# The first MLP's tiles one token group after the other, no partial sums in DRAM, a new issue order, operands at other addresses

## The chip, the cores and the metric

The kernel runs on one core of a Trainium2 chip. The metric is the device time of one execution in microseconds (us); lower is better. A measurement is the median of a few runs.

## The reference

Attention with a window of 64 keys, then two MLPs on the 2304 tokens (4 batches of 576, 8 heads of 64; width 512).

```python
attn = softmax(where((rel >= 0) & (rel < 64), q @ k.T / 8, -1e9)) @ v        # per batch and head
x = attn, heads side by side                                                 # 2304 x 512
h = x @ w_in;  x = (h * tanh(softplus(h))) @ w_out                           # 512 -> 2048 -> 512
h = x @ w_in2;  solu = h * softmax(h)                                        # 512 -> 1024
x = ((solu - mean) / sqrt(var + 1e-6) * g_ln) @ w_out2                       # 1024 -> 512
```

## The kernel before

The tokens are cut into five groups of 512, 512, 512, 384 and 384. For each group the attention of its blocks of 64 tokens (in pairs) leaves its output in a tile `xt` (two buffers, so group j+2 needs the one that group j gives back), split into a high and a low half. The first MLP goes through items `(j, f, a, b)` in the list `its`: group j, column tile f of sixteen of 128 columns, tokens a to b of the group. An item is 12 matmuls of `pe_m1` (L950, into `ps_h`), Mish on ScalarE (L960), the split of its result into two halves `g` (on ScalarE or VectorE, L423, L427, L443), then 8 matmuls of `pe_m2` (L984) and 4 of `pe_m2l` (L995) that add to the group's four accumulators `x2`, a PSUM bank each. All of them read both operands as fp32r, one pass.

The order of the items before is: group 0, tiles 0 to 3, in two halves of 256 tokens; group 0, tiles 4 to 7; group 1, tiles 0 to 7; then tiles 8 to 15 of group 0 and of group 1; then groups 2, 3 and 4 with sixteen tiles each. So groups 0 and 1 each close their accumulators twice: behind tile 7 the sums go to DRAM (`part_d`, `store_x2`), and behind tile 15 they are read back (`load_part`) and added on VectorE (`evac_part`, L1010). The finished group goes to DRAM (`x2d`) for the second MLP.

The weights come as 32-bit halves of 64-bit numbers in pieces of one or two tiles (`c_load`, L481, with two staging buffers `st`). ScalarE or GpSimd scale the words (L491 to L500), VectorE joins them (L508, L516), and they are split into a high half (L423, L427) and a low half (L443). From the third group on, attention transposes its scores in blocks through DRAM (`blocks_out`, L375, then `blocks_in`, L381), and so does the second MLP for its second product.

The second MLP takes two tiles of 128 tokens at a time: seven products of 6 matmuls (`b_p`, L1118) with `xs` (on the right side of SBUF) or, for every second pair, `xs_w` (in a weight buffer on the left side) as the stationary operand and `w_in2` as the moving one, then SoLU and the norm, then 24 matmuls of `b_m4` (L1235) for each of the 18 tiles.

Nothing is scheduled by the compiler. A planner in the program (`Schedule`) has all steps with their costs and what they come after; in `run` it takes, step by step, the one that its own clock lets start first, and among those within `PATIENCE` the one with the lowest number in `RANK`. The order in which it takes them is the order on each engine's queue. All DMAs are issued by SP.

SBUF is filled from both sides. From the left, starting at byte 1152 of a partition: `ident`, `mask_n`, `mask_0` (512 bytes each), `g_sb` (32 bytes), the weight buffers, `st`, `xt`, `mc`, `g`, `xs` of the evacuation. From the right, downward from byte 229344: the attention's tiles, later those of the second MLP. All large tiles have multiples of 128 bytes.

## Time and profile before

| | us |
|---|---|
| median of 3 runs | 669.59 |
| lowest and highest run | 665.54, 669.97 |
| the profiled execution, whole | 667.13 |
| its span, first to last instruction | 665.4 |
| PE busy (of the span) | 649.1 |
| DVE, ACT, POOL busy | 423.6, 348.3, 40.9 |

PE is TensorE's matmuls, PEld its weight loads (beside PE), DVE is VectorE, ACT is ScalarE, POOL is GpSimd, SP issues DMAs (its queue is SPq). Busy time is the union of an engine's instructions. Matmuls are pipelined, so the time of one in a stream is read from the distance between starts, as the chain gives it, and not from its own duration.

### The profile page before, as it was taken

The numbers are of one execution on the slowest core, as the hardware profiler recorded it, in microseconds if no ns is written. First come the engines' busy times: TensorE is split into PE (matmuls) and PEld (weight loads), VectorE is DVE, ScalarE is ACT, GpSimd is POOL, SyncE is SP. The second block draws the span as 40 slices with busy tenths as digits, with TensorE's granted clock in tenths as the row PEclk, the third lists the DMA queues.
The fourth block names the chain that finished last, engine by engine and source line by source line (L and its number), as shares of the span: only waits on it lengthen the run. The fifth ranks groups of instructions, "written<-read, shape, count | busy, mean of one in ns | idle before, by whom it ended". The sixth has DMA issues, their size and how long they took to land.

```text
span 665.4 us, 10569 instructions
## 1 busy us (share of the span) xinstructions
PE 649.1 (98%) x4089; PEld 556.8 (84%) x4089; DVE 423.6 (64%) x741; ACT 348.3 (52%) x616; POOL 40.9 (6%) x63
## 2 busy tenths in 40 slices
PE   8899999999999989999999999999998999999997
PEld 6688888878888878788899999999886888788886
DVE  4778887876356656321115655776687988879751
ACT  5989775544344434232123545655576555657532
POOL 2412000000000001000000010000011001110100
PEclk9999999999999999999999999999999999999999
DMA  8874565576068453020044345602216555554562
GB/s 333 332 279 166 163 214 199 181 272 207 1 205 254 145 185 131 32 64 1 0 159 159 108 117 173 210 13 95 80 37 154 189 159 158 173 160 139 174 178 95
DMA packets 56962, 101.36 MB, mean 152 GB/s; under 512 B 5072, under 2 KB 30672, under 8 KB 56912
## 3 DMA queue, kind: packets, MB, share of 16 engines
q1 hardware_dynamic: 56912, 100.69, 46.5%
q8 instruction: 32, 0.52, 0.3%
q14 instruction: 18, 0.15, 0.1%
HBM read 74.45 MB, written 26.21 MB: 151 GB/s over the span
## 4 chain that ended last, share of the span: by engine, by line
PE 77%; DMA 10%; DVE 6%; ACT 3%; SPq 2%; issue 1%; POOL 0%; ACTq 0%; DVEq 0%
PE ps_h L950 26%; PE x L984 18%; PE po L1235 10%; PE x L995 9%; PE pb L1118 9%; DMA t_d<-s 3%; PE ps_o L903 2%; PE ps_s L741 2%; DMA h_b<-t_d 2%; DMA t_d<-y_b 2%; DMA st<-w_in 1%; SPq L381 1%; DMA room_q<-qk 1%; DMA pt<-t_d 1%; DMA xr<-x2d 1%
## 5 line engine op out<-in xcount | busy, mean ns | idle before, releaser
L950 PE MATMUL ps_h<-xt,w 128*128 128x512 f32 (+2 forms) x1008 | 205.4, 359 | 1.2 <-ACT mc L960 1.0
L950 PEld LDWEIGHTS ps_h<-xt,w 128*128 128x128 f32 x1008 | 177.2, 188 | 23.1 <-ACT mc L960 1.9
L984 PE MATMUL x<-g,w 128*128 128x512 f32 (+2 forms) x672 | 146.5, 359 | 1.0 <-DVE g L427 0.6
L984 PEld LDWEIGHTS x<-g,w 128*128 128x128 f32 x672 | 118.8, 188 | 16.3 <-ACT g L423 1.1
L443 DVE SCALAR_TENSOR_TENSOR g<-mc,g 128x512 fp32r<-128x512 f32 (+2 forms) x84 | 51.5, 618 | 94.8 <-ACT g L423 94.3
L1235 PE MATMUL po<-w,lz 128*128 128x512 f32 x432 | 101.4, 391 | 2.6 <-ACT lz L1215 2.5
L1235 PEld LDWEIGHTS po<-w,lz 128*128 128x128 f32 x432 | 80.6, 188 | 21.4 <-ACT lz L1215 4.6
L960 ACT ACTIVATE mc<-ps_h 128x512 f32<-128x512 f32 (+2 forms) x84 | 44.8, 535 | 98.5 <-PE ps_h L950 94.5
L995 PE MATMUL x<-g,w 128*128 128x512 f32 (+2 forms) x336 | 80.8, 362 | 0.0
L423 ACT ACTIVATE g<-mc 128x512 fp32r<-128x512 f32 (+2 forms) x68 | 39.2, 578 | 60.4 <-PE x L995 59.3
L995 PEld LDWEIGHTS x<-g,w 128*128 128x128 f32 x336 | 59.4, 188 | 7.9 <-issue 1.0
L1118 PE MATMUL pb<-w,xs 128*128 128x512 f32 x210 | 51.1, 395 | 0.0
L1118 PEld LDWEIGHTS pb<-w,xs 128*128 128x128 f32 x210 | 39.4, 188 | 9.2
L1118 PE MATMUL pb<-w,xs_w 128*128 128x512 f32 x168 | 39.8, 390 | 0.0
L1118 PEld LDWEIGHTS pb<-w,xs_w 128*128 128x128 f32 x168 | 31.5, 188 | 6.7
L1215 ACT ACTIVATE lz<-h_b 128x512 fp32r<-128x512 f32 x36 | 21.3, 626 | 29.6 <-DMA h_b<-t_d 19.4
L1219 DVE TENSOR_TENSOR lz<-h_b,lz 128x512 fp32r<-128x512 f32 x36 | 24.0, 686 | 17.3 <-ACT lz L1215 17.2
L508 DVE SCALAR_TENSOR_TENSOR st<-st 128x1024 uint32<-128x1024 uint32 x22 | 26.9, 1224 | 10.8 <-ACT st L493 9.2
L844 POOL TENSOR_TENSOR s<-s,rs 128x1024 f32<-128x1024 f32 x6 | 11.5, 1923 | 354.0 <-DMA x2d<-xs 187.3
L435 ACT ACTIVATE v_b<-pb 128x512 f32<-128x512 f32 x33 | 19.6, 595 | 20.0 <-PE pb L1118 18.2
L500 ACT ACTIVATE st<-st 128x1024 uint32<-128x1024 uint32 x22 | 25.4, 1156 | 6.3 <-DMA st<-w_out 6.3
L1150 ACT ACTIVATE e<-h_b,nm 128x1024 f32<-128x1024 f32 x18 | 20.7, 1151 | 9.1 <-DVE nm L1141 8.9
(133 smaller groups left out, 712.5 us busy)
## 6 DMA issues: line engine op xcount, KB each, us to landing
qk<-qk SPq DMA_DIRECT2D x32, 512.0 KB, 5.2
st<-w_out SPq DMA_DIRECT2D x12, 1024.0 KB, 5.7
st<-w_in SPq DMA_DIRECT2D x10, 1024.0 KB, 6.0
t_d<-y_b SPq DMA_DIRECT2D x18, 512.0 KB, 2.8
h_b<-t_d SPq DMA_DIRECT2D x72, 128.0 KB, 3.2
v<-v SPq DMA_DIRECT2D x32, 256.0 KB, 3.7
t_d<-s SPq DMA_DIRECT2D x10, 512.0 KB, 3.3
pt<-t_d SPq DMA_DIRECT2D x40, 128.0 KB, 3.1
```

Of the source, the lines that this page charges most:

```text
L423: nc.scalar.activation(out=hi, in_=x, func=ACTF.Copy, scale=1.0 if g is None else g)
L443: nc.vector.scalar_tensor_tensor(out=lo, in0=x, scalar=1.0 if g is None else g, in1=hi.bitcast(F32), op0=ALU.mult, op1=ALU.subtract)
L500: nc.scalar.activation(out=w, in_=w, func=ACTF.Copy, scale=0.9325 * 2.0**-29)
L508: nc.vector.scalar_tensor_tensor(out=lw, in0=uw, scalar=3, in1=lw, op0=ALU.logical_shift_left, op1=ALU.bitwise_or)
L950: nc.tensor.matmul(out=ps[:, :n], lhsT=w[:, a, k, fs], rhs=x[:, b, k, a0:a1], start=(idx == 0), stop=(idx == len(terms) - 1),)
L960: nc.scalar.activation(out=c[:, :n], in_=ht.pop(i)[:, :n], func=ACTF.Mish)
L984: nc.tensor.matmul(out=acc[j][m][:, a0:a1], lhsT=w[:, a, f % 4, m * P:(m + 1) * P], rhs=g[:, 0, :n], start=(i in opens and a == 0), stop=F ...
L995: nc.tensor.matmul(out=acc[j][m][:, a0:a1], lhsT=w[:, 0, f % 4, m * P:(m + 1) * P], rhs=g[:, 1, :n], start=False, stop=i in closes,)
L1118: nc.tensor.matmul(out=ps, lhsT=x[:, a, ix, k, :], rhs=w[:, k, :], start=first and n == 0, stop=n == len(terms) - 1, skip_group_check=not ...
L1215: nc.scalar.activation(out=lt[t][:, 0, fs].rearrange(SPLIT, i=4), in_=pst[t][:, :, fs], func=ACTF.Copy)
L1219: nc.vector.tensor_tensor(out=lt[t][:, 1, fs].rearrange(SPLIT, i=4), in0=pst[t][:, :, fs], in1=lt[t][:, 0, fs].bitcast(F32).rearrange(SPLI ...
L1235: nc.tensor.matmul(out=po[t], lhsT=lz[:, a, f, :], rhs=wt["w4", f // 4][:, b, f % 4, :], start=(c == 0 and idx == 0), stop=(c == 2 and idx ...
```

## The change

- `its` has all sixteen tiles of group 0 (the first four in halves, as before), then all of group 1, then the rest as before. `CUT`, `part_d`, `load_part` and `evac_part` go; `opens` and `closes` hold five sets of accumulators in place of seven. The places of attention beside the items follow from `its`, and group 2's due times (`BESIDE_AT`) are new.
- `RANK` is new from end to end, and some costs in the planner are new.
- `g_sb` is opened behind the left side's attention tiles in place of among the constants, a tile `pad` of 96 bytes is the first on the right side, and the tile `warm`, read twice in place of once by the warm-up matmuls, is half as large. So the left side's tiles start 32 bytes lower and the right side's 96 bytes lower.

```diff
@@ -26,7 +26,6 @@
 BLK = 64
 LD = 2
 HALF = 4
-CUT = 8
 N_T = 16
 SPLIT = "p f (i c) -> p i f c"
 LAG = 3
@@ -73,7 +72,7 @@
 FIRST_AT = (-247.536, -138.103, 26.663)
 W_STEP = 5.104
 M4_LATER = -89.542
-BESIDE_AT = ((74.191, 100.532), (62.075, 50.39), (-14.947, 89.638), (16.431, 50.986), (-8.343, 27.444))
+BESIDE_AT = ((74.191, 100.532), (62.075, 50.39), (4.0, 24.0), (16.431, 50.986), (-8.343, 27.444))
 BESIDE_PE = 2.411
 PATIENCE = 0.031
 SLACK = 41.257
@@ -93,86 +92,84 @@
 
 
 RANK = (
...
@@ -359,12 +356,9 @@
     x2d = [dram.tile([P, KD, n], F32, name=f"x2d{j}") for j, n in enumerate(GROUPS)]
-    part_d = [dram.tile([P, KD, n], F32, name=f"part{j}") for j, n in enumerate(GROUPS[:2])]
-
     ident = const.tile([P, P], F32, name="ident")
     mask_n = const.tile([P, P], F32, name="mask_n")
     mask_0 = const.tile([P, P], F32, name="mask_0")
-    g_sb = const.tile([P, NF2], F32, name="g_sb")
@@ -408,8 +402,13 @@
     st_p = actx.enter_context(tc.tile_pool(name="st", bufs=2))
     x_p = actx.enter_context(tc.tile_pool(name="x", bufs=2))
     m_p = actx.enter_context(tc.tile_pool(name="m", bufs=2))
+    g_p = actx.enter_context(tc.tile_pool(name="g_ln", bufs=1))
+    g_sb = g_p.tile([P, NF2], F32, name="g_sb")
     ps_x2 = actx.enter_context(tc.tile_pool(name="ps_x2", bufs=KD, space=PSUM))
     ps_h = actx.enter_context(tc.tile_pool(name="ps_h", bufs=2, space=PSUM))
+
+    pad = ctx.enter_context(tc.tile_pool(name="pad", bufs=1, side="right"))
+    pad.tile([P, 24], F32, name="pad")
     tctx = ExitStack()
     ectx = ExitStack()
     ld_p = tctx.enter_context(tc.tile_pool(name="ld", bufs=LD, side="right"))
@@ -586,10 +585,8 @@
     n = GROUPS[0] // 2
     its = [(0, f, o, o + n) for o in (0, n) for f in range(HALF)]
-    its += [(0, f, 0, 2 * n) for f in range(HALF, CUT)]
-    its += [(1, f, 0, GROUPS[1]) for f in range(CUT)]
-    its += [(j, f, 0, GROUPS[j]) for j in range(2) for f in range(CUT, NF)]
-    its += [(j, f, 0, GROUPS[j]) for j in range(2, NG) for f in range(NF)]
+    its += [(0, f, 0, 2 * n) for f in range(HALF, NF)]
+    its += [(j, f, 0, GROUPS[j]) for j in range(1, NG) for f in range(NF)]
     NI = len(its)
     first_of = {}
     for i, it in enumerate(its):
@@ -682,7 +679,7 @@
     def warm_up():
-        w = sm_p.tile([P, 256], BF16, tag="warm", name="warm", bufs=1)
+        w = sm_p.tile([P, P], BF16, tag="warm", name="warm", bufs=1)
         nc.vector.memset(w, 0.0)
         room["warm"] = w
         zeros(ps_h.tile([P, 512], F32, tag="h", name="ps_w"), N_WARM)
@@ -690,7 +687,10 @@
     def zeros(ps, n):
         w = room["warm"]
         for _ in range(n):
-            nc.tensor.matmul(out=ps[:, :256], lhsT=w[:, :P], rhs=w, start=True, stop=True)
+            nc.tensor.matmul(
+                out=ps[:, :256].rearrange("p (a b) -> p a b", a=2), lhsT=w, rhs=w.unsqueeze(1).to_broadcast([P, 2, P]),
+                start=True, stop=True,
+            )
     def bridge(ps):
@@ -927,8 +927,8 @@
-    opens = {i for i, (j, f, a, b) in enumerate(its) if a == 0 and (f == 0 or (f == CUT and j < 2))}
-    closes = {i for i, (j, f, a, b) in enumerate(its) if f == NF - 1 or (f == CUT - 1 and j < 2)}
+    opens = {i for i, (j, f, a, b) in enumerate(its) if a == 0 and f == 0}
+    closes = {i for i, (j, f, a, b) in enumerate(its) if f == NF - 1}
     ht, ct, gt = {}, {}, {}
     acc = {}
@@ -997,20 +997,7 @@
                 start=False, stop=i in closes,
             )
-    out_t, xs_t = {}, {}
-
-    def load_part(j, m):
-        out_t[m] = m_p.tile([P, GMAX], F32, tag="xs", name="xs", bufs=KD)
-        nc.sync.dma_start(out=out_t[m][:, :GROUPS[j]], in_=part_d[j][:, m, :])
-
-    def evac_part(i, m):
-        j, f, _, _ = its[i]
-        n = GROUPS[j]
-        s = out_t.pop(m)
-        nc.vector.scalar_tensor_tensor(
-            out=s[:, :n], in0=acc[j][m][:, :n], scalar=1.0, in1=s[:, :n], op0=ALU.mult, op1=ALU.add
-        )
-        xs_t[m] = s
+    xs_t = {}
     def evac_x2(e, i, m):
         j, f, _, _ = its[i]
@@ -1025,7 +1012,7 @@
     def store_x2(i, m):
         j, f, _, _ = its[i]
         n = GROUPS[j]
-        nc.sync.dma_start(out=(x2d if f == NF - 1 else part_d)[j][:, m, :], in_=xs_t.pop(m)[:, :n])
+        nc.sync.dma_start(out=x2d[j][:, m, :], in_=xs_t.pop(m)[:, :n])
     with tc.manual_schedule():
@@ -1382,7 +1369,7 @@
             mx = step(dict(dve=0.84), t + offs[2], a_max0, n, after=[qk], new=[s, nm], uses=[S, s, nm, room_s])
             e0 = step(dict(act=0.70), t + offs[3], a_exp0, n, (0, 1), after=[mx], uses=[S, s, nm, room_s], table="exp")
             e1 = step(dict(act=0.70), t + offs[4], a_exp0, n, (2, 3), after=[e0], uses=[S, s, nm], table="exp")
-            r = step(dict(dve=0.35), t + offs[5], a_norm, n, after=[e1], new=[rs], uses=[nm, rs])
+            r = step(dict(dve=0.4), t + offs[5], a_norm, n, after=[e1], new=[rs], uses=[nm, rs])
             mu = step(COSTS["mul0"], t + offs[5], a_mul, n, after=[r], uses=[s, rs], two=True)
             tr = step(dict(pe=0.434), t + offs[6], a_tr, n, after=[mu], new=[T], uses=[s, T])
             cp = step(COSTS["pt0"], t + offs[7], a_pt, n, after=[tr], uses=[T, s])
@@ -1405,7 +1392,7 @@
                 mx = step(dict(dve=1.37), t + offs[2], a_max, n, after=[qk], new=[nm], uses=[S, nm])
             else:
                 qk = step(dict(pe=0.88), t + offs[0], a_qk, n, after=lks + pv_of_old, new=[S], uses=ks + [S], mode="qk")
-                sc = step(dict(dve=1.23 if n < N_T else 1.55), t + offs[1], a_scale, n, after=[qk, masks, mask_x] + moved[-1:], new=[s], uses=[S, s])
+                sc = step(dict(dve=1.23 if n < N_T else 1.42), t + offs[1], a_scale, n, after=[qk, masks, mask_x] + moved[-1:], new=[s], uses=[S, s])
                 mx = step(dict(dve=1.2), t + offs[2], a_max, n, after=[sc], new=[nm], uses=[s, nm])
             if n < NM:
                 ex = step(dict(act=1.55), t + offs[4], a_exp2, n, range(NP), after=[mx], new=[s], uses=[S, s, nm], table="exp")
@@ -1418,7 +1405,7 @@
                 su = step(dict(dve=1.23), t + offs[3], a_sub, n, after=[mx], uses=[s, nm])
                 ex = step(dict(act=1.03), t + offs[4], a_exp, n, after=[su], uses=[s], table="exp")
                 sm = step(dict(dve=1.2), t + offs[5], a_sum, n, after=[ex], uses=[s])
-            r = step(dict(dve=0.35), t + offs[5], a_norm, n, after=[sm], new=[rs], uses=[rs])
+            r = step(dict(dve=0.4), t + offs[5], a_norm, n, after=[sm], new=[rs], uses=[rs])
             mu = step(COSTS["mul"], t + offs[6], a_mul, n, after=[r], uses=[s, rs], two=True)
             if n < N_T:
                 tr = step(dict(pe=0.87), t + offs[7], a_tr, n, after=[mu] + pv_last[-1:], new=[T], uses=[s, T])
@@ -1427,10 +1414,10 @@
                 c = [c0, c1]
             else:
                 T = Buf("s2")
-                bl = step(dict(dve=1.13), t + offs[7], a_blocks, n, after=[mu], uses=[s])
+                bl = step(dict(dve=1.25), t + offs[7], a_blocks, n, after=[mu], uses=[s])
                 td = Buf("td")
-                mo = step(dict(dma=1.4), t + offs[8], a_out, n, after=[bl], new=[td, T], uses=[s, td])
-                c0 = step(dict(dma=2.0), t + offs[8], a_in, n, after=[mo], uses=[T, td])
+                mo = step(dict(dma=1.5), t + offs[8], a_out, n, after=[bl], new=[td, T], uses=[s, td])
+                c0 = step(dict(dma=2.6), t + offs[8], a_in, n, after=[mo], uses=[T, td])
                 moved.append(mo)
                 c, s = [c0, c0], T
             finish(n, t, offs[9:], mu, (ws, s), O, c)
@@ -1465,22 +1452,13 @@
             last_m2[:] = [m2]
             m1_of[i], m2_of[i] = m1, m2
             if i in closes:
-                loads, outs_ = [], []
                 for m in range(KD):
-                    part = j < 2 and f == NF - 1
                     xs = Buf("xs")
-                    if part:
-                        loads.append(step(dict(dma=0.7), o[4] - 2.5, load_part, j, m, after=[part_of[j][m], m1_of[i - 3]] + last_out, new=[xs], uses=[xs]))
-                    ev = step(
-                        dict(dve=0.15 + 0.4 * k) if part else COSTS["x2"], o[4] + 1.2, evac_part if part else evac_x2, i, m, after=[m2] + loads[m:m + 1], new=[] if part else [xs],
-                        uses=[xs, acc_of[j][m]],
-                    )
+                    ev = step(COSTS["x2"], o[4] + 1.2, evac_x2, i, m, after=[m2], new=[xs], uses=[xs, acc_of[j][m]])
                     sto = step(dict(dma=0.7), o[4] + 1.3, store_x2, i, m, after=[ev], uses=[xs])
-                    outs_.append(sto)
-                    (part_of if f == CUT - 1 and j < 2 else done_of).setdefault(j, []).append(sto)
-                last_out[:] = outs_
-
-        acc_of, part_of, done_of, last_m2, last_out = {}, {}, {}, [], []
+                    done_of.setdefault(j, []).append(sto)
+
+        acc_of, done_of, last_m2 = {}, {}, []
         U0 = PRE_STEP
         PRE = -(N0 - 1) * U0 - max(PRE_AT) - 0.02
         for n in range(N0):
@@ -1563,7 +1541,7 @@
                     after = after + [vs_[bank][-1]]
                 if ps_:
                     after = after + [ps_[-1]]
-                q = step(dict(pe=1.362), a + P_AT[3], b_p, u, i, after=after, new=[bk[bank]] if first else [], uses=[bk[bank], xs_])
+                q = step(dict(pe=1.4), a + P_AT[3], b_p, u, i, after=after, new=[bk[bank]] if first else [], uses=[bk[bank], xs_])
                 ps_.append(q)
                 xs_last[u % 2] = [q]
                 got[i] = q
@@ -1578,7 +1556,7 @@
                 t = 2 * u + i
                 after = [x for n in vn for x in vs_["v", n]] + ([got[q]] if q is not None else []) + ([cs[t, 0]] if c else [])
                 cs[t, c] = step(
-                    dict(dve=0.84), a + P_AT[5], b_c, u, i, c, after=after + [ob2], new=[hb[t]] if c == 0 else [],
+                    dict(dve=0.72), a + P_AT[5], b_c, u, i, c, after=after + [ob2], new=[hb[t]] if c == 0 else [],
                     uses=[hb[t]] + ([bk[bank]] if bank is not None else []),
                 )
                 for n in vn:
@@ -1595,13 +1573,13 @@
             sq = step(dict(act=1.25), o[2], b_sq, t, after=[sa], uses=[h, y, st])
             va = step(dict(dve=0.28), o[2], b_var, t, after=[sq], uses=[st])
             va = step(dict(pool=1.0), o[3], b_pow, t, after=[va], uses=[st])
-            sh = step(dict(dve=0.3), o[3], b_shift, t, after=[va], uses=[st])
+            sh = step(dict(dve=0.2), o[3], b_shift, t, after=[va], uses=[st])
             z = step(dict(dve=0.82), o[3], b_z, t, after=[sh], uses=[h, st])
             Y, lz = Buf("bty"), Buf("blz")
-            tr = step(dict(dve=1.13), o[4], b_tr, t, after=[z, ob2], new=[Y], uses=[h, Y])
+            tr = step(dict(dve=1.25), o[4], b_tr, t, after=[z, ob2], new=[Y], uses=[h, Y])
             td = Buf("td")
-            mo = step(dict(dma=1.4), o[4], b_out_t, t, after=[tr], new=[td], uses=[Y, td])
-            mv = step(dict(dma=2.0), o[4], b_in_t, t, after=[mo], uses=[h, td])
+            mo = step(dict(dma=1.5), o[4], b_out_t, t, after=[tr], new=[td], uses=[Y, td])
+            mv = step(dict(dma=2.6), o[4], b_in_t, t, after=[mo], uses=[h, td])
             h0 = step(dict(act=0.55), o[5], b_hi, t, 0, after=[mv], new=[lz], uses=[h, lz])
             l0 = step(dict(dve=0.69), o[5], b_lo, t, 0, after=[h0], uses=[h, lz], two=True)
             h1 = step(dict(act=0.55), o[5], b_hi, t, 1, after=[h0], uses=[h, lz])
```

## Rows read from the trace of the kernel before

**Rows 1.** Part 1 of the page: busy us (share of the span) xinstructions.

```profile
PE 649.1 (98%) x4089; PEld 556.8 (84%) x4089; DVE 423.6 (64%) x741; ACT 348.3 (52%) x616; POOL 40.9 (6%) x63
```

**Rows 2.** Stretches; for each engine busy us and (xinstructions), then clock, DMA share, GB/s.

```profile
0.00:33.00 33.00, 27.38 (x336) 21.97 (x336) 20.52 (x43) 25.62 (x87) 10.88 (x22) 1.00 0.90 335
33.00:129.00 96.00, 94.19 (x735) 81.33 (x732) 79.05 (x98) 72.07 (x142) 5.69 (x3) 1.00 0.59 198
129.00:235.90 106.90, 106.64 (x739) 87.08 (x739) 65.99 (x92) 45.13 (x58) 0.00 (x0) 1.00 0.57 185
...
462.00:640.00 178.00, 175.43 (x777) 144.20 (x776) 145.10 (x345) 107.20 (x185) 20.34 (x36) 1.00 0.47 143
640.00:665.40 25.40, 21.60 (x96) 17.55 (x94) 6.10 (x9) 6.12 (x11) 0.00 (x0) 0.99 0.37 115
```

**Rows 3.** Chain of work that ended last: start, us, engine, tile, line, xcount.

```profile
39.79 1.44 PE ps_h L950 x12
...
94.08 19.04 PE ps_h L950 x84
...
412.20 12.48 PE ps_h L950 x72
```

**Rows 4.** Waits of PE, longest first: us in total, times, longest; two of nine, and the last.

```profile
PE po L1235 <- ACT lz L1215: 2.5, 2, 1.7
PE ps_o L903 <- DMA pt<-t_d: 2.1, 2, 1.9
...
PE x L984 <- ACT g L423: 0.4, 1, 0.4
```

**Rows 5.** Part 6 of the page, DMA issues of the partial sums.

```profile
part<-xs SPq DMA_DIRECT2D x8, 256.0 KB, 4.8
xs<-part SPq DMA_DIRECT2D x8, 256.0 KB, 5.0
```

**Rows 6.** Groups by line and form: the add of a partial sum on DVE.

```profile
L1010 DVE SCALAR_TENSOR_TENSOR xs<-x,xs 128x512 f32<-128x512 f32 x8 | 5.3, 686 | 0.1
```

**Rows 7.** Stretches from 0, matmuls of line L950 alone: length, busy us, (xcount).

```profile
0.00:129.20 129.20, 46.65 (x240) 1.00 0.67 233
...
0.00:150.70 150.70, 57.96 (x288) 1.00 0.69 238
0.00:156.30 156.30, 63.52 (x312) 1.00 0.69 238
```

**Rows 8.** DVE in order of time, last step of a weight piece: start us, us.

```profile
73.21 1.22 DVE L443 SCALAR_TENSOR_TENSOR w<-st,w 128x1024 fp32r<-128x1024 f32 x1
...
86.96 1.22 DVE L443 SCALAR_TENSOR_TENSOR w<-st,w 128x1024 fp32r<-128x1024 f32 x1
...
127.15 1.22 DVE L443 SCALAR_TENSOR_TENSOR w<-st,w 128x1024 fp32r<-128x1024 f32 x1
...
133.36 1.23 DVE L443 SCALAR_TENSOR_TENSOR w<-st,w 128x1024 fp32r<-128x1024 f32 x1
```

**Rows 9.** PE in order of time, three rows that have a wait in brackets.

```profile
246.09 1.15 PE L903 MATMUL ps_o<-pt,v 128*64 128x64 f32 x32 [1.89 <-DMA pt<-t_d]
...
507.48 7.87 PE L1235 MATMUL po<-w,lz 128*128 128x512 f32 x32 [1.67 <-ACT lz L1215]
...
566.61 3.93 PE L1235 MATMUL po<-w,lz 128*128 128x512 f32 x16 [0.87 <-ACT lz L1215]
```

**Rows 10.** Waits of SP's queue (issuing of DMAs).

```profile
SPq L481 <- DVE w L443: 60.8, 10, 12.4
```

**Rows 11.** PE in order of time at the start of the second MLP.

```profile
473.78 8.56 PE L1118 MATMUL pb<-w,xs 128*128 128x512 f32 x36
482.18 9.71 PE L1118 MATMUL pb<-w,xs_w 128*128 128x512 f32 x42
491.73 8.56 PE L1118 MATMUL pb<-w,xs 128*128 128x512 f32 x36
```

**Rows 12.** Part 5 of the page, the product with xs.

```profile
L1118 PE MATMUL pb<-w,xs 128*128 128x512 f32 x210 | 51.1, 395 | 0.0
```

158 rows, old and new, of the table RANK are left out of this document.

## The prediction, made before the changed kernel was run

> **What bounds the kernel now.** I read the page's busy shares first, then the 20-us-and-longer stretches, then the list of what TensorE waited for, then the chain of work that ended last. TensorE is busy 649.1 of 665.4 us [rows 1], at a granted clock of 1.00 in every stretch, the higher of its two levels (2.4 GHz) [rows 2]. The chain, too, is TensorE work for long stretches without a break [rows 3]. So the reader should not look for a big wait; the question is what TensorE's own 649 us consist of and where its 16 us of idle time lie. By the stretches 5.6 us of idle time lie ahead of 33 us, 1.8 between 33 and 129 us, 2.6 in the second MLP, and 3.8 behind the last matmul (the output's copy and store) [rows 2]. The list of waits holds nine entries of 0.4 to 2.5 us each, and none of them names a partial sum, its load or its store [rows 4].
>
> The matmuls themselves: there are 84 passes of 24 in the first MLP, 378 in the second one's first product and 432 in its last, 2826 in all, of which 1866 have 512 columns, 768 have 384 and 192 have 256 (from the loops). Where the chain runs through many of them in a row, one takes 19.04/84 = 226.7 ns at 512 columns, 12.48/72 = 173.3 ns at 384 and 1.44/12 = 120 ns at 256 [rows 3]. Each is 13.3 ns above its columns at 2.4 GHz (213.3, 160.0, 106.7). Sum: 1866 x 0.2267 + 768 x 0.1733 + 192 x 0.120 = 579 us. The diff leaves every one of these 2826 in place, with the same shapes. So the time can only move by the idle time, by the 13.3 ns, or by new waits.
>
> **Part 1, no partial sums.** Removed: 8 stores and 8 loads of 256 KB [rows 5], and the 8 adds on VectorE (5.3 us busy, 0.69 each) [rows 6]; the other evacuations stay. No wait of TensorE is put down to them [rows 4], VectorE is busy for only 79 of the 96 us ahead of 129 us and less behind [rows 2]. I cost this at 0; the cover is the TensorE queue itself, and without it one add would be worth 0.7 us. Closing a set of accumulators happens five times in place of seven. There TensorE bridges the evacuation with the next tiles' first matmuls, and no wait shows there either: 0.
>
> **Part 2, the order of the tiles.** This is where a new wait could come from. Tile 8 of group 0 now follows tile 7 directly, so weight pieces for tiles 8 to 15 are wanted earlier. Before, tile 8's first matmul is number 241 of its line, at 129.2 us, tile 12's number 289, at 150.7, tile 14's number 313, at 156.3 [rows 7]. The last step of converting the pieces (the subtraction that writes the low half) starts at 86.96 us for tiles 8 and 9 and at 127.15 and 133.36 us for tiles 12 to 15 of w_in, 1.2 us each [rows 8]. So before there are 41, 22 and 22 us of slack.
>
> After: tile 8 comes where group 1's first tile stood, at 93.8 us, or some 6 us earlier, since group 1's attention (four pairs of blocks, each three bursts on TensorE, of which the last is 1.15 us [rows 9]; by that size some 3.4 us a pair, an estimate) is now spread over twice as many tiles. That is 88 to 94 us against 88.2 us. From there two tiles cost TensorE 2 x 24 x 0.2267 = 10.9 us, while two tiles need two pieces, one of each matrix, and the pieces come every (133.36 - 73.21)/9 = 6.7 us (ten such rows from the first to the last of [rows 8]), 13.4 us for both. The pace is set by a ring: two staging buffers, a load that waits for the last VectorE step of the piece before (60.8 us of such waits in the queue that issues the DMAs [rows 10]). Supply is thus a little slower than demand and the slack is eaten. TensorE's work from 33 us to the end of group 0 is 8 half tiles of 24 x 0.120 = 23.0 us, 12 tiles of 5.44 = 65.3 us and about 15 us of attention (four to five pairs): earliest end 136 us. With the last piece in at 134.6 us and the second products of two tiles (5.4 us) behind it, the end is 140 us: up to 3.5 us lost. Against that, TensorE may run group 1's first products meanwhile, w_in's last pieces can swap with w_out's, and the VectorE work of group 1's attention moves later. Bounds: 0 and +3.5 for this; I take +1.5. Queued behind a late weight on TensorE are the second products, the evacuation of group 0, and with it nothing that is due soon.
>
> Group 2's attention wants the x buffer that group 0 frees with its last first product. That comes some 40 us earlier than now; no wait of TensorE shows there, so: 0.
>
> **Part 3, the ranks and the corrected costs.** The issue order is new everywhere; it can't be read from the diff. What can be said: three of TensorE's waits stand behind the block transposes through DRAM, 1.89, 1.67 and 0.87 us [rows 9], 4.4 us in all, and the planner's costs for just these two DMA steps go up (1.4 to 1.5, 2.0 to 2.6 of its units), so that it leaves more room there. Bounds: all of it gained (-4.4), or other waits of that size in their place (0, and as much again on the far side, +4.4). I take half: -2.2. The other changed costs move no instruction by themselves.
>
> **Part 4, aligned places.** Worked out from the tiles' sizes: g_sb's 32 bytes in front put every operand of the left side 32 bytes past a multiple of 128, and the right side's tiles lie 96 bytes past one; after the change both lie on multiples of 128. The second MLP's first product shows that place can matter: with xs (right side) as the stationary operand, 36 matmuls take 482.18 - 473.78 = 8.40 us, 233.3 ns each, with xs_w (left side) 42 take 9.55 us, 227.4 ns, and the moving operand is the same [rows 11]. There are 210 of the slow kind [rows 12]: moving xs to the better place is worth 210 x 5.9 ns = 1.2 us. For the other 2600 no row shows a place at a multiple of 128, so the price per matmul is bounded by 0 and 13.3 ns (all of what is above the columns), and a loss is bounded by the 6.6 ns that the worse place shows. I take 0: the 13.3 ns are the same at three widths, as a fixed cost of changing weights would be. So -1.2 here.
>
> A page of the Trainium skill speaks against even that: SBUF — State Buffer, section Specifications (TRN2), has lines of 16 bytes, on which both places start cleanly; by it the 1.2 us would not be gained. The row above contradicts it as far as it goes: 233.3 against 227.4 ns.
>
> **Sum**, against the profiled execution's own time (667.13 us: its span of 665.4 and 1.7 around it): 667.1 + 1.5 - 2.2 - 1.2 = 665.2. The three runs shown are 665.5, 669.6 and 670.0, the profiled one lies inside them, so I name the same figure for a run: 665. Against the median (669.6) that is -0.7%, less than the 1% or so that a measurement of this kernel can tell from no change. With the bounds (0 to +3.5; -4.4 to +4.4; 0 to -1.2; and the 4.4 us by which runs of one kernel differ) the forecast's own range is 658 to 673.
>
> **Rival A, the whole TensorE stream gets faster.** If the 13.3 ns come from operands that straddle something at 32 bytes past 128, all 2826 matmuls gain. For it: the same operation on the same moving operand costs 5.9 ns more at another place [rows 11]. Against it: the excess doesn't grow with the moving operand's length (13.3 ns at 256 and at 512 columns [rows 3]). Half of it is 2826 x 6.7 ns = 19 us: 646 us. All of it is 38 us: 627.
>
> The Trainium skill (TensorE: Matmul & The Clock Gate, section Back-to-back issue gap) gives N/2.4 + 2.5 ns for a warm matmul, 215.8 ns at 512 columns where the trace has 226.7. By that rule the excess of 10.8 ns is not the array's, and if the places cause it the estimate is 667 - 31 = 636 us; no run shown yet has such a matmul of this type.
>
> **Rival B, slower: the weights of tiles 8 to 15 come late.** The ring of two staging buffers is the mechanism, group 0 between 88 and 140 us the place. It decides as soon as supply falls more than one piece (6.7 us) behind the clock it keeps now, for instance because the new ranks put group 1's attention or its loads ahead of a conversion. Two pieces late cost 13 us less the filler: 675 to 680 us. For it: no slack is left by the count above, VectorE and ScalarE are busy 82 and 75% there [rows 2]. Against it: both have 17 to 24 us free in that stretch, and attention is pushed out of it.
>
> **Rival C, it does not do what it says:** the order changes, but xs stays slow or other operands land in the worse phase (2600 x 6.6 ns = 17 us, 682 us).
>
> **Chances.** Forecast 0.57, A 0.26, B 0.14, C 0.03. The likeliest is the forecast: 665. To hold 8 in 10 the range takes in A's milder half and B's beginning: 644 to 676. Faster by over 1% (under 662.9): A, and a quarter of the forecast, 0.41. Slower by over 1% (over 676.3): most of B and C, 0.12. Within: 0.47.
>
> **What would show it.** In the changed profile: no DMA named part and no new wait of TensorE near the ends of groups 0 and 1; the line of the first product without a gap from tile 7 to tile 8 near 90 us, but with waits on VectorE's weight steps if B holds; the pb rows alike for xs and xs_w near 227 ns; 84 matmuls of 512 columns in 19.04 us again, and not in 18.5 or less as under A; the waits behind the transposes shorter. The prediction fails if the pitch of 226.7 ns moves, since it is multiplied by 2826, or if TensorE's idle time in 88 to 140 us exceeds 5 us.

## The result and the profile after

| | before | after |
|---|---|---|
| median of 6 runs each | 668.49 | 657.17 |
| lowest and highest run | 664.76, 669.97 | 656.93, 658.10 |
| the profiled execution, whole, and its span | 667.13, 665.4 | 658.10, 656.3 |

The ratio of after to before is 0.984 [0.982, 0.986]: 1.6% faster, where 0.7% was forecast. The time is 8 us under the figure named and just under the forecast's own range (658 to 673). It lies inside the wide range (644 to 676) only by the room made for rival A, which did not come: that is luck. The runs also lie closer together: 1.2 us between the lowest and the highest in place of 5.2.

First the busy times of after (part 1 of the page), which answer to [rows 1]:

```profile
PE 645.3 (98%) x4086; PEld 556.5 (85%) x4086; DVE 411.8 (63%) x722; ACT 352.3 (54%) x625; POOL 42.0 (6%) x64
```

The stretches of after, with the columns of [rows 2] (the last one is shorter, since the span is):

```profile
0.00:33.00 33.00, 27.61 (x315) 22.46 (x316) 22.53 (x45) 24.87 (x85) 12.67 (x23) 1.00 0.91 335
33.00:129.00 96.00, 95.26 (x815) 81.76 (x814) 82.69 (x101) 80.86 (x152) 4.29 (x2) 1.00 0.67 232
129.00:235.90 106.90, 106.90 (x686) 87.64 (x685) 52.40 (x76) 43.88 (x60) 3.83 (x2) 1.00 0.40 134
235.90:462.00 226.10, 226.10 (x1438) 208.16 (x1437) 106.06 (x150) 97.17 (x148) 1.92 (x1) 1.00 0.28 94
462.00:640.00 178.00, 177.74 (x790) 147.34 (x789) 145.53 (x350) 101.85 (x176) 19.30 (x36) 1.00 0.47 151
640.00:656.30 16.30, 11.67 (x52) 9.14 (x50) 2.59 (x4) 3.65 (x7) 0.00 (x0) 0.97 0.25 82
```

The stretch of before that [rows 2] leaves out:

```profile
235.90:462.00 226.10, 223.82 (x1418) 204.69 (x1417) 106.80 (x155) 92.13 (x136) 3.95 (x2) 1.00 0.31 102
```

TensorE's idle time ahead of 33 us goes from 5.6 to 5.4 us, between 33 and 129 us from 1.8 to 0.7, between 235.9 and 462 us from 2.3 to 0, in the second MLP from 2.6 to 0.3, and behind 640 us from 3.8 to 4.6. The chain of after answers to [rows 3]:

```profile
145.55 13.60 PE ps_h L950 x60
...
372.94 6.24 PE ps_h L950 x36
```

13.60/60 is 226.7 ns and 6.24/36 is 173.3 ns, the pitch of before to the tenth. What TensorE waits for in after, nine of ten rows, answers to [rows 4]:

```profile
PE ps_t L690 <- ACT s L771: 1.6, 1, 1.6
PE ps_t L856 <- POOL room_s L844: 1.2, 1, 1.2
PE ps_o L903 <- DVE room_s L436: 1.0, 1, 1.0
PE ps_w L690 <- DVE warm L683: 1.0, 1, 1.0
PE ps_s L733 <- DVE nm L750: 0.4, 1, 0.4
PE ps_h L950 <- ACT mc L960: 0.3, 1, 0.3
PE po L1222 <- ACT lz L1202: 0.3, 1, 0.3
PE x L984 <- ACT g L422: 0.2, 1, 0.2
...
PE ps_h L950 <- DVE w L442: 0.2, 1, 0.2
```

The reader should see what is missing: the 2.1 us behind the transposes of attention (`ps_o` on `pt<-t_d`) have no row, and the 2.5 us of `po` on `lz` are down to 0.3. The four longest that are left stand in the opening (`s`, `room_s`, `warm`). The last row is the whole stall for a weight. Two more rows of before, beside that of 0.4 in [rows 4], are waits of the first MLP for its own activations:

```profile
PE ps_h L950 <- ACT mc L960: 1.0, 1, 1.0
PE x L984 <- DVE g L427: 0.6, 1, 0.6
```

Where the 9.1 us between the two spans lie is read from four starts. Two rows of before, TensorE in order of time:

```profile
32.98 1.22 PE L950 MATMUL ps_h<-xt,w 128*128 128x256 f32 x8
...
629.69 31.91 PE L1235 MATMUL po<-w,lz 128*128 128x512 f32 x140
```

and the same view of after:

```profile
31.21 3.00 PE L950 MATMUL ps_h<-xt,w 128*128 128x256 f32 x23
...
468.27 8.36 PE L1105 MATMUL pb<-w,xs 128*128 128x512 f32 x36
476.47 9.68 PE L1105 MATMUL pb<-w,xs_w 128*128 128x512 f32 x42
...
629.68 21.99 PE L1222 MATMUL po<-w,lz 128*128 128x512 f32 x96
```

| from ... to | before | after | difference |
|---|---|---|---|
| start to the first matmul of the first MLP | 32.98 | 31.21 | -1.8 |
| to the second MLP's own stream (473.78 of [rows 11], 468.27) | 440.80 | 437.06 | -3.7 |
| to the end of the last matmul (661.60, 651.67) | 187.82 | 183.40 | -4.4 |
| to the end of the span | 3.80 | 4.63 | +0.8 |

The first row has no transpose through DRAM in it: the first one is issued at 157 us in before and at 131 us in after. In the second row 2.1 us are the waits behind `pt<-t_d` and 1.3 the waits for `mc`, `g` and a weight (2.0 in before, 0.7 in after). In the third, 2.2 are those of `po` on `lz` and 1.2 the product with `xs`, whose busy time falls from 51.1 us [rows 12] to 49.9:

```profile
L1105 PE MATMUL pb<-w,xs 128*128 128x512 f32 x210 | 49.9, 389 | 0.0
```

With the opening (1.8) and the later end (0.8) that names 7.8 of the 9.1. The other 1.3 have no row. A matmul lasts 389 ns by its own duration and its neighbour starts after 227, so a break of up to 0.16 us counts as busy time and not as a wait; that the 1.3 consist of such breaks is not shown. What sets the waits is the experiments' question.

### The profile page after: what moved, and what is told of

The parts are those of the page before. It is cut to its first block, busy times and chain, and to the rows that moved or that the text cites. A ratio compares the mean times of both kernels' runs of the same rounds, so it can differ in the third digit from the quotient of the medians.

```text
span 656.3 us, 10523 instructions
## 1 busy us (share of the span) xinstructions
PE 645.3 (98%) x4086; PEld 556.5 (85%) x4086; DVE 411.8 (63%) x722; ACT 352.3 (54%) x625; POOL 42.0 (6%) x64
## 4 chain that ended last, share of the span: by engine, by line
PE 92%; ACT 3%; DVE 2%; issue 1%; DMA 1%; SPq 0%; ACTq 0%
PE ps_h L950 30%; PE x L984 20%; PE po L1222 13%; PE pb L1105 12%; PE x L995 10%; PE ps_o L903 2%; PE ps_s L741 2%; DMA t_d<-y_b 1%; PE ps_t L856 1%; PE ps_w L690 1%; PE ps_s L723 0%; DMA h_b<-t_d 0%; ACT s L771 0%; DVE nm L812 0%; DVE nm L814 0%
## 5 line engine op out<-in xcount | busy, mean ns | idle before, releaser
L950 PE MATMUL ps_h<-xt,w 128*128 128x512 f32 (+2 forms) x1008 | 205.5, 359 | 0.5 <-ACT mc L960 0.3
L950 PEld LDWEIGHTS ps_h<-xt,w 128*128 128x128 f32 x1008 | 177.1, 188 | 22.0 <-ACT mc L960 0.5
L422 ACT ACTIVATE g<-mc 128x512 fp32r<-128x512 f32 (+2 forms) x79 | 45.1, 573 | 38.0 <-PE x L995 36.4
L1105 PE MATMUL pb<-w,xs 128*128 128x512 f32 x210 | 49.9, 389 | 0.0
L844 POOL TENSOR_TENSOR s<-s,rs 128x1024 f32<-128x1024 f32 x7 | 13.8, 1977 | 351.8 <-ACT xt L434 207.2
L434 ACT ACTIVATE v_b<-pb 128x512 f32<-128x512 f32 x30 | 17.8, 597 | 23.4 <-PE pb L1105 17.1
L1156 ACT ACTIVATE e<-h_b,st 128x1024 f32<-128x1024 f32 x18 | 20.7, 1148 | 9.4 <-DVE st L1150 9.3
```

The lines of the kernel that those rows point to most:

```text
L422: nc.scalar.activation(out=hi, in_=x, func=ACTF.Copy, scale=1.0 if g is None else g)
L950: nc.tensor.matmul(out=ps[:, :n], lhsT=w[:, a, k, fs], rhs=x[:, b, k, a0:a1], start=(idx == 0), stop=(idx == len(terms) - 1),)
L1105: nc.tensor.matmul(out=ps, lhsT=x[:, a, ix, k, :], rhs=w[:, k, :], start=first and n == 0, stop=n == len(terms) - 1, skip_group_check=not ...
```

## The experiments

| kernel | us, median | lowest, highest | ratio to before on the same chip |
|---|---|---|---|
| p0_after | 657.17 | 656.92, 658.07 | 0.986 [0.983, 0.988] |
| p1_old_places | 658.88 | 658.33, 660.52 | 0.988 [0.985, 0.991] |
| p2_both96 | 658.23 | one run | |
| p3_right64 | 658.46 | one run | |
| q1_old_order_new_costs | 658.65 | 657.54, 659.35 | 0.989 [0.987, 0.992] |
| q2_new_order_old_costs | 662.29 | 660.26, 664.46 | 0.994 [0.991, 0.997] |
| q3_before_new_places | 665.17 | 662.80, 666.97 | 0.998 [0.996, 1.000] |
| q4_after_with_parts | 657.28 | 656.51, 659.36 | 0.988 [0.985, 0.991] |
| r1_dma_costs_only | 656.71 | 656.46, 658.27 | 0.983 [0.980, 0.985] |
| r2_engine_costs_only | 663.84 | 661.65, 665.25 | 0.993 [0.990, 0.996] |
| r3_longer_dma | 657.82 | 656.47, 660.11 | 0.984 [0.981, 0.987] |
| r4_after_again | 657.65 | 656.68, 658.65 | 0.983 [0.980, 0.986] |

Before ran beside each set: median 666.83 for p (7 runs), 666.77 for q (19 runs, 663.75 to 671.32), 668.20 for r (8 runs).

**The places.** Four kernels with after's issue order, which differ only in where the left and the right side of SBUF begin.

> The changed kernel once more, as the yardstick for the next three on the same chip. Both theories: 657 us within 1.

p1 puts the old places back:

```diff
+    g_sb = const.tile([P, NF2], F32, name="g_sb")
...
-    pad.tile([P, 24], F32, name="pad")
```

> The changed kernel with g_sb among the constants again and without the pad: left side 32 bytes past a multiple of 128, right side 96. The issue order is untouched. Theory 1 (places matter for xs alone): the product with xs back at 233 ns per matmul, all others at 226.7, and 210 x 6 ns = 1.3 us slower, 658.4 us. Theory 2 (much of the 11 us gained comes from aligned places elsewhere, DMAs and the other engines too): 661 us or more.

p2 puts left and right side both 96 bytes past a multiple of 128:

```diff
+    g_sb = const.tile([P, NF2], F32, name="g_sb")
+    const.tile([P, 16], F32, name="more")
...
-    pad.tile([P, 24], F32, name="pad")
```

> The changed kernel with both sides 96 bytes past a multiple of 128, so every operand lies at the place that xs had before. If that place itself is bad: 233 ns for all 512-column matmuls, some 17 us slower (674 us). If what counts is where the stationary operand lies relative to the moving one: 226.7 ns everywhere, xs included, and 657 us.

p3 puts the right side 64 bytes past one, and leaves the left at 0:

```diff
-    pad.tile([P, 24], F32, name="pad")
+    pad.tile([P, 8], F32, name="pad")
```

> The changed kernel with the right side 64 bytes past a multiple of 128 and the left on it: xs stands to its moving operand as before the change (64 apart), but at another place. Relative theory: the product with xs at 233 ns again, about +1.3 us. Theory of the place itself (96 past is bad): 227 ns or something between.

The start of the second MLP on TensorE, in order of time; 36 products with `xs`, then 42 with `xs_w`. After again (p0):

```profile
469.12 8.36 PE L1105 MATMUL pb<-w,xs 128*128 128x512 f32 x36
477.32 9.68 PE L1105 MATMUL pb<-w,xs_w 128*128 128x512 f32 x42
```

With the old places (p1):

```profile
469.73 8.56 PE L1102 MATMUL pb<-w,xs 128*128 128x512 f32 x36
478.13 9.71 PE L1102 MATMUL pb<-w,xs_w 128*128 128x512 f32 x42
```

Both sides at 96 (p2):

```profile
468.59 8.36 PE L1103 MATMUL pb<-w,xs 128*128 128x512 f32 x36
476.79 9.68 PE L1103 MATMUL pb<-w,xs_w 128*128 128x512 f32 x42
```

Right at 64, left at 0 (p3):

```profile
467.64 8.56 PE L1105 MATMUL pb<-w,xs 128*128 128x512 f32 x36
476.04 9.71 PE L1105 MATMUL pb<-w,xs_w 128*128 128x512 f32 x42
```

From start to start 36 take 8.20, 8.40, 8.20 and 8.40 us: 227.8 ns each in p0 and p2, 233.3 in p1 and p3. So it isn't the place as such. The pair is slow when the stationary operand on the right and the moving one on the left stand 64 bytes apart within 128 (96 against 32, 64 against 0), and fast when they stand alike (0 and 0, 96 and 96), aligned or not. The other streams of 512 columns keep 226.7 ns at all four. The old places cost 658.88 - 657.17 = 1.7 us, the new ones alone give q3 1.6 (below): the 1.2 of the count, and no more than noise beside it. The single runs of p2 and p3 (658.23 and 658.46) can't part the two; the start-to-start times do.

**Order of tiles against ranks and costs.** A fixed list of ranks does not fit other costs, so q1, q2 and the r kernels have a `RANK` of their own, searched with the planner's clock for the end of the last step.

q1 is the kernel before (its order of tiles, its partial sums), with the new places, every cost of the change, and a `RANK` for them; two of the twelve changed lines:

```diff
-            r = step(dict(dve=0.35), t + offs[5], a_norm, n, after=[sm], new=[rs], uses=[rs])
+            r = step(dict(dve=0.4), t + offs[5], a_norm, n, after=[sm], new=[rs], uses=[rs])
...
-                c0 = step(dict(dma=2.0), t + offs[8], a_in, n, after=[mo], uses=[T, td])
+                c0 = step(dict(dma=2.6), t + offs[8], a_in, n, after=[mo], uses=[T, td])
```

> The kernel before (old order of tiles, partial sums in DRAM) with the changed kernel's planner costs and places, and an own list of ranks, searched with the planner under those costs until its clock ended at 652.3, as it does for the changed kernel (652.6). Theory R (the gain is an issue order planned with costs that the chip keeps): 657 us within 2, and TensorE's waits behind the block transposes gone. Theory O (the gain is the order of the tiles and the partial sums): 662 us or more.

q2 is the kernel after, with every old cost and a `RANK` for them:

```diff
-            r = step(dict(dve=0.4), t + offs[5], a_norm, n, after=[sm], new=[rs], uses=[rs])
+            r = step(dict(dve=0.35), t + offs[5], a_norm, n, after=[sm], new=[rs], uses=[rs])
...
-                c0 = step(dict(dma=2.6), t + offs[8], a_in, n, after=[mo], uses=[T, td])
+                c0 = step(dict(dma=2.0), t + offs[8], a_in, n, after=[mo], uses=[T, td])
```

> The changed kernel (new order of tiles, new places) with the old planner costs and an own list of ranks, searched under these until the planner's clock ended at 651.1, earlier than in either kernel. Theory R: the chip doesn't keep it: 661 to 667 us, with waits behind the transposes and the weights. Theory O: 656 to 658 us.

q3 is the kernel before, with its `RANK` and costs, at the new places:

```diff
-    g_sb = const.tile([P, NF2], F32, name="g_sb")
...
+    pad.tile([P, 24], F32, name="pad")
```

> The kernel before with the new places alone (g_sb moved, pad, half the warm tile), its issue order untouched. Places worth 1.3 us: 0.998 of the kernel before, 665.5 to 667 us beside its median, the product with xs at 227 ns. If places also matter to its waits: 0.995 or less.

q4 is the kernel after, with traffic like that of the partial sums:

```diff
+        if j < 2 and f == 7:
+            for m in range(KD):
+                nc.sync.dma_start(out=part_d[j][:, m, :], in_=xt[j][:, 0, m, :n].bitcast(F32))
+        if j < 2 and f == 12:
...
+                nc.sync.dma_start(out=out_t[m][:, :n], in_=part_d[j][:, m, :])
...
+            nc.vector.scalar_tensor_tensor(
+                out=s[:, :n], in0=acc[j][m][:, :n], scalar=1.0, in1=s[:, :n], op0=ALU.mult, op1=ALU.add
+            )
```

> The changed kernel with the traffic of the partial sums put back: for groups 0 and 1, 4 stores of 256 KB behind tile 7, 4 loads behind tile 12, and the evacuation as an add on VectorE with the loaded data. What is stored is the attention's output, so the sum that it adds is not the reference's. The issue order is otherwise untouched. Forecast of part 1 (costs nothing): 657 us within 1. Rival: the loads and stores delay what SP issues next and the transposes behind it, 659 us or more.

q1 has the old order of tiles and all of the partial sums, and 658.65 us, nearly the whole gain. q2 has the new order and 662.29. q4 carries 8 stores and 8 loads more than after, with 8 adds in place of copies, and takes 657.28. So neither the order of the tiles nor the partial sums make the difference. What TensorE waits for in q2 (first row; the ninth, `pt<-t_d`, has 0.4):

```profile
PE po L1223 <- ACT lz L1203: 2.6, 3, 1.3
```

and in q3, where the waits of before are back (first, second and fourth row):

```profile
PE ps_s L747 <- DMA qk<-qk: 2.8, 2, 1.5
PE po L1241 <- ACT lz L1221: 2.2, 2, 2.0
...
PE ps_o L909 <- DMA pt<-t_d: 1.6, 2, 1.1
```

In q1 neither `lz` nor `pt<-t_d` has a row (a load of a partial sum has one, of 0.6). That points to the costs, but there are two sorts of them: those of engines' steps and those of the two transposes through DRAM.

q3 has the issue order of before, so its trace is a second sample of the same waits. The same four products wait behind the transposes: in attention 0.47 and 1.12 us (0.26 and 1.89 in before), in the second MLP 1.97 and 0.28 (1.67 and 0.87), 3.8 us in all beside 4.7. New in q3 are the waits for `qk`. Behind the longer one, TensorE in order of time:

```profile
53.37 1.10 PE L747 MATMUL ps_s<-qk 64*64 64x128 f32 x30 [1.49 <-DMA qk<-qk]
54.57 5.99 PE L956 MATMUL ps_h<-xt,w 128*128 128x256 f32 x24
```

and TensorE alone in stretches (length, busy us, xinstructions, clock, DMA share, GB/s):

```profile
52.00:54.00 2.00, 0.64 (x24) 1.00 0.91 263
...
56.00:58.00 2.00, 2.00 (x9) 0.50 0.88 358
```

TensorE was busy for 0.64 of the 2 us from 52 to 54; from 56 to 58 us its granted clock was 0.50, the lower of its two levels (1.2 GHz). The 24 matmuls behind the wait take 5.8 us to the next start, and 4.3 in before, where the clock stays at 1.00. So this wait of 1.5 us took about as much again with it, which no list of waits shows.

**Which costs.** Both of the next two are the kernel before with its order of tiles, its partial sums and the new places; they differ in their costs and in the `RANK` searched for them.

r1 changes the times of `a_out` and `a_in`, and of `b_out_t` and `b_in_t` alike:

```diff
-                mo = step(dict(dma=1.4), t + offs[8], a_out, n, after=[bl], new=[td, T], uses=[s, td])
-                c0 = step(dict(dma=2.0), t + offs[8], a_in, n, after=[mo], uses=[T, td])
+                mo = step(dict(dma=1.5), t + offs[8], a_out, n, after=[bl], new=[td, T], uses=[s, td])
+                c0 = step(dict(dma=2.6), t + offs[8], a_in, n, after=[mo], uses=[T, td])
```

> The kernel before (its tile order, its partial sums) with the new places, all of the old costs except the two of the transposes through DRAM (1.5 and 2.6), and an issue order searched anew for these costs; the planner's own end is 651.8. Theory D, the gain comes from the room that the planner now leaves behind the transposes: 658 to 660 us as with all the new costs (658.65), no wait behind pt<-t_d or lz above 0.5 us, and single runs within 2 to 3 us of each other. Theory E, it comes from the corrected times of VectorE's and TensorE's steps: 662 to 665 us, with waits of 1 us and more on lz, nm, mc or g. If any freshly searched order would do (theory L): 658 to 660 here and in the run with the engines' costs alone.

r2 changes only those of engines' steps (norm 0.4, scale 1.42, block transpose 1.25, first product 1.4, `b_c` 0.72, shift 0.2), one of which is:

```diff
-                bl = step(dict(dve=1.13), t + offs[7], a_blocks, n, after=[mu], uses=[s])
+                bl = step(dict(dve=1.25), t + offs[7], a_blocks, n, after=[mu], uses=[s])
```

> The same kernel, but with the new costs of the engines' steps (norm, scale, block transpose, first product, c, shift) and the old ones of the transposes through DRAM (1.4 and 2.0); searched anew, planner's own end 652.0. Theory D: 662 to 665 us, waits of 1 to 2.5 us on lz or pt<-t_d, runs spread by 4 us. Theory E: 658 to 660 us and no such wait. Theory L (luck of a fresh order): 658 to 660 here too.

r1 takes 656.71 us, 1.3 under what theory D gave, and r2 663.84: 7.1 apart, with ranges that don't touch. The first product of the first MLP, two of the products of attention that read a transposed tile, and the last two streams of the second MLP, TensorE in order of time, in r2:

```profile
31.08 1.70 PE L956 MATMUL ps_h<-xt,w 128*128 128x256 f32 x12 [0.24 <-DVE xt L932]
...
190.88 1.15 PE L909 MATMUL ps_o<-pt,v 128*64 128x64 f32 x32 [1.79 <-DMA pt<-t_d]
...
225.87 1.15 PE L909 MATMUL ps_o<-pt,v 128*64 128x64 f32 x32 [1.20 <-DMA pt<-t_d]
...
644.02 5.73 PE L1241 MATMUL po<-w,lz 128*128 128x512 f32 x24 [0.17 <-ACT lz L1221]
650.39 5.73 PE L1241 MATMUL po<-w,lz 128*128 128x512 f32 x24 [0.63 <-ACT lz L1221]
```

and in r1 the first product, one of the ten products of attention that read a transposed tile (none has a bracket) and the last stream:

```profile
28.64 1.68 PE L956 MATMUL ps_h<-xt,w 128*128 128x256 f32 x12
...
189.03 1.15 PE L909 MATMUL ps_o<-pt,v 128*64 128x64 f32 x32
...
629.70 21.24 PE L1241 MATMUL po<-w,lz 128*128 128x512 f32 x93
```

The last matmul of r1 ends at 629.70 + 21.24 = 650.94, of r2 at 650.39 + 5.73 = 656.12. Of these 5.2 us 2.4 lie in the opening, ahead of any transpose through DRAM, and 2.7 behind it. The waits behind the transposes are 3.8 us in r2 (3.0 in attention, 0.8 on `lz`) and none in r1, which has a wait of 0.75 for `qk` instead. The transfers themselves are alike in the median. From issue to landing, all DMAs that write or read `t_d` (the two halves of every transpose), in r1:

```profile
DMA to landing us min/median/max: 2.4/2.9/5.4
```

in r2:

```profile
DMA to landing us min/median/max: 2.4/2.9/7.4
```

and in before:

```profile
DMA to landing us min/median/max: 2.5/3.1/6.5
```

So the typical DMA of the faster kernel is no faster; what is longer is the plan's time for it. The planner adds 1.6 us for the landing to each cost of a DMA (`delay` in `Schedule`), so a round trip of one store and four loads has 1.4 + 1.6 + 2.0 + 1.6 = 6.6 us under the old costs and 7.3 under the new. In before the issuing of one of the loads (ns, lowest, median, highest) and the medians from issue to landing (part 6 of the page) are:

```profile
L381 SPq DMA_DIRECT2D pt<-t_d x40: 318/428/441, 160.6 to 397.0; - x40
t_d<-s SPq DMA_DIRECT2D x10, 512.0 KB, 3.3
pt<-t_d SPq DMA_DIRECT2D x40, 128.0 KB, 3.1
```

The store, three issues of loads and the landing of the fourth load make 3.3 + 3 x 0.43 + 3.1 = 7.7 us, an estimate from these rows; with the second MLP's 2.8 and 3.2 it is 7.3. The old plan was thus short of the typical round trip by 0.7 to 1.1 us, and the new one about meets it.

r3 is the kernel after with longer times still, and r4 after itself beside it:

```diff
-                mo = step(dict(dma=1.5), t + offs[8], a_out, n, after=[bl], new=[td, T], uses=[s, td])
-                c0 = step(dict(dma=2.6), t + offs[8], a_in, n, after=[mo], uses=[T, td])
+                mo = step(dict(dma=1.8), t + offs[8], a_out, n, after=[bl], new=[td, T], uses=[s, td])
+                c0 = step(dict(dma=3.2), t + offs[8], a_in, n, after=[mo], uses=[T, td])
```

> The kernel after with the planner's times of the two transposes through DRAM raised once more (1.8 and 3.2 in place of 1.5 and 2.6), searched anew; planner's own end 652.6, as that of after (652.6). Theory D, if more room still helps: 655.5 to 656.5 us; if the room of after is enough: 657 to 658. Theory E: 657 to 658, the order of engines' work being as good as before.

> The kernel after, unchanged, beside the three others on the same chip: 657.2 us (656.9 to 658.1), by every theory.

r3 takes 657.82 us beside 657.65 of after: a further 0.9 us of room gains nothing. r1 at 656.71 is the fastest median of the twelve, but its runs and those of after overlap. No version here beats the changed kernel by more than a measurement can tell.

**All lists together.** Each list of ranks is one find of a search, so r1 against r2 alone could be luck. But four lists were made under the longer times of the transposes (after, q1, r1, r3) and take 656.7 to 658.7 us; three have the old times (q3, q2, r2) and take 662.3 to 665.2. By chance alone all four would lie under all three once in 35 times. The waits of TensorE behind `pt<-t_d` and `lz` are 0 to 0.3 us in the profiles of the four and 3.0 to 3.8 in those of the three.

## Where the prediction was right, and the step that failed

**Right: what TensorE's 645 us are, and that rival A fails.** The pitch stayed 226.7 and 173.3 ns with every operand at a multiple of 128, and the 2826 matmuls kept their price but for the 210 with `xs`. The Trainium skill's N/2.4 + 2.5 ns (TensorE: Matmul & The Clock Gate, section Back-to-back issue gap), which that section gives for an isolated matmul and not for a stream with weight loads as here, is met at no place that p0 to p3 tried: 226.7 ns, not 215.8.

**Right: Part 1 at 0.** No DMA names `part`, VectorE is busy 411.8 in place of 423.6 us, and putting the traffic back costs nothing (q4).

**Right: Part 4 at -1.2.** Counted -1.2, read from the busy time as -1.2, measured -1.7 (p1) and -1.6 (q3). The Trainium skill's lines of 16 bytes (SBUF — State Buffer, section Specifications (TRN2)) don't account for it: all the places here start on such lines, and two of the four are slow.

**Part 2, +1.5: the stall did not come, and rival B with it.** The count of L950 in after, from 0, answers to [rows 7]:

```profile
0.00:79.62 79.62, 24.07 (x145) 20.73 (x145) 1.00 0.79 285
```

Tile 8 of group 0 (matmul 145) starts at 79.62 us, even earlier than the 88 to 94 forecast, and the second products of group 0 end at 137.6 (forecast 136 to 140). But the conversion moved as well. The last step of the last weight piece on VectorE in after, the answer to [rows 8]:

```profile
124.18 1.22 DVE L442 SCALAR_TENSOR_TENSOR w<-st,w 128x1024 fp32r<-128x1024 f32 x1
```

The last piece is in at 125.4 us, 9 us earlier than before. I had held the old times of the conversion fixed while everything around it was ordered anew, and counted the filler (attention and group 1's first products) at less than it does: TensorE waits 0.2 us for a weight, at 38 us, and is idle for none of the 52 us from 88 to 140. The order is worth 0 in the other direction too: in one set of runs r1, with the old order and the partial sums, has 656.71 us and after 657.65.

**Part 3, -2.2: this is the step that failed.** The mechanism was named, but its size was put at about half, and what the new list of ranks does elsewhere was put at nothing. "I take half" of the three waits was the value, "all of it gained (-4.4)" the lower bound. By the profiles the change without the places gives 9.1 - 1.2 = 7.9 us, by the medians 11.3 - 1.6 = 9.7: beyond the bound. The 7.9 are made up as follows.

- The waits behind the transposes: 4.3 gained (2.1 and 2.2), nearly all of them and not half.
- Waits in other places, 2.3: the opening is 1.8 us shorter and the first MLP's waits for `mc`, `g` and a weight 1.3, the end is 0.8 longer. "The other changed costs move no instruction by themselves" was true and beside the point: with an order made anew they do. A new list helps even under the old costs: q2 has 0.994 of before where q3 has 0.998, some 3 us, an estimate over two orders of tiles. The corrected costs of engines' steps add nothing visible to that (r2, 0.993).
- 1.3 that no row names.

Split by the ratios, with 668 us as one: the places 0.2% (1.4 us), a new list of ranks 0.4% (3), the order of the tiles and the partial sums 0, and the transposes' times 0.4 to 1.0% (3 to 7 us): r2 against q1 gives 0.993 and 0.989, r2 against r1 0.993 and 0.983. q2 against the 657.3 to 657.7 us of q4 and r4 has 5 us, but there all costs differ. q1 and r1 share the transposes' times and differ by 1.9 us, so a searched order carries about that much luck. That the transposes' times matter is shown by the four lists against the three, and for 3.0 to 4.7 us by the waits in the profiles of before, q3, q2 and r2. What makes up the rest of the upper figure stays open. One candidate is the clock: 14 of the 34 runs of before that stand beside the experiments have a mean granted clock of 0.994 to 0.997, and all 14 runs of after one of 0.998 or more. It does not explain the medians, since before without those runs is only 0.1 to 0.8 us faster. Landings that are late in other runs are another; before and q3, two traces of one order, wait at the same four products, so no trace shows it.

Two smaller readings were off. The forecast's own range, 658 to 673, is not what its bounds add up to: these give 661.5 to 675 before any spread between runs. And the granted clock is 0.99 in the last stretch of [rows 2], not 1.00; that changes nothing here.

The Trainium skill gives a rule for a DMA's duration (DMA: Bandwidth & Descriptors, section Anatomy of one DMA — SWDGE (gpsimd) path): 2.0 us and the bytes over 436 GB/s, for the path of GpSimd, where here SP issues. By it a store of 512 KB would be an estimated 3.2 us. The pages of before, after, r1 and r2 have medians of 2.7 to 3.7 for the stores to `t_d`, so it agrees for the typical one; the longest of 5.4 to 7.4 it doesn't have. The planner's 1.4 + 1.6 = 3.0 us for the store was near that too; it was the four loads that it had short (2.0 + 1.6 = 3.6, against 4.4 from the rows above).

Rival C didn't come either: `xs` is at 227 ns and nothing is slower. The forecast's sign held. So did its statement that the time can move only by idle time, new waits and the 13.3 ns, as far as the rows go: 1.3 us of the 9.1 have none.

## What to carry to other kernels

When an order of issue is fixed in advance, compare the plan's time for each long step with the trace, above all where it scatters (here a round trip through DRAM, each of its DMAs 2.4 to 7.4 us): a plan about 1 us short of the typical round trip cost 3 to 7 us on the chip, and 0.9 us beyond it gained nothing. The waits listed for the step in question (4.4 us here) don't bound what a new order gains, because it moves other waits too, and a wait can bring a fall of the clock with it that the list does not have (q3). The 16 transfers of the partial sums, 256 KB each, for which TensorE did not wait, gave nothing when they went.

## What was not expected of the hardware

A matmul of 512 fp32r columns takes 233.3 in place of 226.7 ns in a stream when its stationary and its moving operand lie 64 bytes apart within 128, at two pairs of places (96 and 32, 64 and 0), and not when they lie alike (0 and 0, 96 and 96). Other distances, and whether the sides of SBUF matter, weren't tried.
